# Chunk attention and a phase MLP on one core: one copy for q and k, token weights cast in the load queue, and a new order of steps

## The chip, the core and the metric

The kernel runs on one core of a Trainium2 chip. A core has TensorE (PE; its weight loads are shown as PEld), VectorE (DVE), ScalarE (ACT), GpSimd (POOL) and SyncE (SP), and 16 DMA engines. POOL issues the loads that change the type on their way (the software queue), SP issues stores, plain copies inside SBUF and DMA transposes. The metric is device time in microseconds of one execution; the median over runs of the same program is compared.

## The reference

For batch 8, 8 heads, 576 positions and head size 64, attention is taken inside chunks of 64 positions. Its output x, 576 x 512 for each batch, goes through a layer that mixes tokens by two weight matrices and channels by one:

```python
scores = scale * np.matmul(q_c, k_c.transpose(0, 1, 2, 4, 3))   # chunks of 64
attn = softmax(scores)
x = (attn @ v_c), heads joined                                   # (8, 576, 512)
theta = x @ w_theta
zr, zi = x * np.cos(theta), x * np.sin(theta)
y = einsum('ts,bsd->btd', w_tok_r, zr) + einsum('ts,bsd->btd', w_tok_i, zi)
u = x + y
return u + np.maximum(u @ w_ch, 0.0)
```

All inputs and the output are float32. The token product of a batch needs all 576 positions of zr and zi of that batch.

## The kernel before

**Tiling.** Two batches form a pair p (0 to 3). A pair has 9 tiles of 128 rows, numbered 0 to 8: 0 to 3 belong to the first batch, 5 to 8 to the second, and tile 4, the middle, holds the last 64 rows of each. The attention steps work on groups of tiles: A is tiles 0 and 1, B is 2 and 3, C is 5 and 6, D is 7 and 8, M is the middle. A step named S.1C is the score step of pair 1, group C; Y.15 is the token product of pair 1, tile 5. A last number in a step's name is the PSUM slot, three double ones ("wide") and two single ones ("thin").

**Steps.** For a group: `q`, `k`, `v` load in float16 through POOL (two DMAs each, of 128 KB written, or 64 KB for M); `T` transposes q and k on PE into one PSUM tile, `tq` copies the q part and `tk` the k part to SBUF (tq on DVE; tk on ACT, for M on DVE); `S` is the scores, `e` the exponential on ACT; `V0` and `V1` multiply by v for four heads each, with the row sum in an extra column; `v0` and `v1` normalise on DVE; `X` transposes x on PE and `x` copies it on ACT, or `Xd` does both as one DMA transpose from SP; `H` multiplies by w_theta; `g` is cosine and sine on ACT; `z` makes zr and zi on DVE; `zm` moves the odd halves of the middle tile by DMA. For a tile: `Y` is the token product, nine matmuls of 512 columns (`Ya`, `Yb`, `Yc` are parts of it for pair 0, first batch), `y` adds x on DVE to give u; `U` transposes u on PE and `u` copies it (even tiles on ACT, odd on DVE), or `Ud` does it by a DMA transpose; `W` multiplies by w_ch, `w` takes the relu and adds u on DVE, `st` stores with two DMAs from SP.

**Weights.** `lt` and `lc` load w_theta and w_ch in float16. `lw.00` loads the real token weights as float32 by SP into `wraw` and `wend`, and `cw` casts them on ACT into `wnat`; `lw.01` loads the imaginary ones through POOL, where the DMA casts. `TW` transposes them on PE in three parts of 30 blocks, each copied by DVE (`twd`) and ACT (`twa`).

**Order.** The order of all steps is written out in one list, ORDER, and every engine works through its own instructions in that order; an engine that waits holds everything behind it. SP's list holds stores, middle moves and transposes mixed. `D` is an idle step: two matmuls (in the old code) on a blank tile whose result nobody reads. Around the places that the prediction speaks of, the old order reads

```
... v1.0B x.0M H.0M.2 V0.0B.0 x.0A ... TW.01.2 z.0A Ya.01.1 ...
... Xd.3D W.24.0 w.22 w.24 W.25.1 H.3D.0 ...
... W.33.1 w.33 st.36 st.34 st.33 U.38.0 u.38 W.38.1 w.38 st.38 D.00.0
```

**Lines.** In the profile: L157 idle matmuls, L174 loads of q and k, L182 loads of v, L198 and L199 the casts, L225 TW, L241 and L243 its copies, L259 T, L277 and L279 tq and tk, L290 S, L303 e, L323 V0 and V1, L335 and L336 v0 and v1, L354 X, L366 x, L375 Xd, L388 H, L404 and L408 g, L417 and L418 z, L431 and L432 zm, L457 Y, L465 y, L474 U, L482 Ud, L489 and L491 u, L497 W, L506 w, L521 st.

Of the kernel before, what the change touches and what calls it, by code (L numbers as in the profile page):

```python
# [9 lines left out]
FP32 = mybir.dt.float32  # L10
FP16 = mybir.dt.float16
# [7 lines left out]
ones.00 D.00.0 lw.00 cw.00 D.00.1 init.00 D.00.0 D.00.1 q.0M q.0B q.0A D.00.0 k.0M  # L19
D.00.1 D.00.0 D.00.1 k.0B TW.00.0 twa.00 k.0A D.00.0 T.0M.1 tk.0M D.00.1 D.00.0 tq.0M  # L20
S.0M.2 e.0M lt.00 T.0B.1 T.0A.2 tk.0A tq.0B D.00.1 tq.0A tk.0B S.0A.2 v.0M V1.0M.1 v.0A
e.0A D.00.0 V0.0M.2 twd.00 S.0B.0 new.00 v1.0M V1.0A.1 v0.0M V0.0A.2 v0.0A v.0B q.1M
v1.0A lw.01 X.0M.2 e.0B V1.0B.0 X.0A.1 v1.0B x.0M H.0M.2 V0.0B.0 x.0A v0.0B q.0C k.1M
v.0C H.0A.1 g.0M X.0B.0 z.0M zm.0M x.0B g.0A TW.02.2 H.0B.0 T.1M.1 twa.02 twd.02 TW.01.2
z.0A Ya.01.1 tk.1M tq.1M g.0B Ya.03.0 twd.01 S.1M.1 k.0C q.0D z.0B q.1B twa.01 Yb.01
T.0C.0 e.1M Yb.03 tq.0C Yc.03 tk.0C S.0C.2 Yc.01 v.1M y.03 k.0D Ya.02.0 e.0C lc.00
V1.0C.1 new.10 V0.0C.0 Yb.02 y.01 v0.0C Yc.02 v.0D v1.0C U.01.1 X.0C.2 u.01 T.0D.0
V0.1M.1 Ya.00.1 Yb.00 x.0C tk.0D y.02 U.02.0 tq.0D v0.1M V1.1M.2 k.1B v1.1M S.0D.1
H.0C.0 u.02 W.02.0 w.02 e.0D V1.0D.2 q.1D V0.0D.1 Yc.00 v1.0D v0.0D g.0C U.03.0 T.1B.2
X.0D.1 X.1M.0 u.03 q.1A y.00 z.0C x.0D W.03.0 w.03 tq.1B x.1M U.00.1 k.1D u.00 H.0D.1  # L30
W.01.1 w.01 tk.1B g.0D z.0D H.1M.0 S.1B.2 k.1A g.1M T.1D.1 tk.1D q.1C v.1B tq.1D e.1B
v.1A W.00.0 k.1C w.00 z.1M Y.05.1 st.01 T.1A.0 tk.1A Y.07.0 v.1D y.05 tq.1A q.2D V0.1B.1
S.1A.2 S.1D.0 e.1D y.07 U.05.1 u.05 Y.06.0 U.07.1 v0.1B e.1A V1.1A.0 y.06 V1.1B.1 T.1C.2
u.07 tk.1C st.02 st.00 v1.1A U.06.0 u.06 tq.1C v1.1B st.03 Y.08.1 X.1B.0 v.1C V0.1A.2
x.1B S.1C.1 W.05.0 V0.1D.0 y.08 v0.1A e.1C v0.1D X.1A.2 x.1A w.05 U.08.1 zm.1M H.1B.1
W.07.0 H.1A.0 g.1B V1.1D.2 w.07 v1.1D Y.04.0 X.1D.1 q.2M z.1B k.2D q.2C g.1A V1.1C.2
T.2D.0 y.04 x.1D z.1A W.06.0 w.06 k.2M tk.2D H.1D.1 v1.1C st.05 u.08 Y.13.0 tq.2D S.2D.2
v.2C g.1D T.2M.0 k.2C y.13 V0.1C.1 Y.10.1 v0.1C X.1C.1 tk.2M tq.2M q.2A e.2D S.2M.0
st.06 T.2C.2 v.2D y.10 st.07 e.2M x.1C new.20 Y.11.0 q.2B v.2M z.1D q.3A W.08.1 tk.2C
k.2B tq.2C k.2A y.11 w.08 S.2C.0 V1.2D.1 U.11.0 e.2C v1.2D H.1C.2 u.11 V0.2D.0 v0.2D  # L40
V0.2M.1 q.3C g.1C U.13.1 v0.2M st.08 Y.12.0 u.13 W.11.1 y.12 X.2D.0 x.2D w.11 V1.2M.1
k.3A V1.2C.2 v1.2M W.13.0 v1.2C U.10.1 V0.2C.1 v0.2C u.10 T.2B.0 st.11 T.2A.2 tk.2A
tk.2B X.2M.1 w.13 tq.2A W.10.1 z.1C U.04.0 u.04 st.13 w.10 H.2D.2 x.2M k.3C tq.2B W.04.0
w.04 H.2M.1 g.2M Y.17.1 v.3C q.3M T.3A.0 X.2C.1 y.17 g.2D v.2B Y.14.0 st.10 z.2M S.2B.2
x.2C tk.3A tq.3A S.2A.1 S.3A.0 y.14 Ud.17 U.12.1 u.12 Y.18.0 y.18 e.2A Y.16.1 k.3M y.16
e.2B W.17.0 v.2A H.2C.1 e.3A w.17 V1.2A.2 v1.2A V0.2A.0 W.12.1 st.04 zm.2M Y.15.0 v0.2A
Ud.14 v.3D w.12 y.15 g.2C V1.2B.2 v1.2B V0.2B.0 v0.2B q.3B X.2A.1 W.14.1 x.2A Ud.18 w.14
st.17 U.16.0 u.16 T.3C.2 X.2B.1 W.16.0 w.16 tk.3C U.15.1 x.2B H.2A.0 u.15 q.3D k.3B
W.15.0 W.18.1 st.12 T.3M.1 k.3D tq.3C z.2C S.3C.2 w.15 w.18 z.2D tq.3M g.2A e.3C st.14
v.3A H.2B.0 Y.27.0 st.16 new.30 v.3M Y.28.1 z.2A tk.3M g.2B y.28 S.3M.2 y.27 z.2B  # L50
V0.3A.1 T.3B.0 Y.26.1 Y.20.0 tq.3B st.18 v0.3A tk.3B Ud.28 V1.3A.0 y.26 e.3M y.20 v1.3A
V1.3M.2 V1.3C.1 v1.3M v1.3C Y.24.1 V0.3C.0 T.3D.2 st.15 Ud.27 S.3B.1 y.24 tq.3D v0.3C
Ud.26 W.26.0 w.26 e.3B W.27.1 v.3B w.27 tk.3D V1.3B.1 V0.3B.0 v0.3B v1.3B S.3D.2 Ud.20
st.27 W.28.0 w.28 Y.21.1 y.21 Xd.3A Ud.21 Y.25.0 V0.3M.0 st.28 v0.3M y.25 e.3D V1.3D.2
V0.3D.1 st.26 Xd.3M Y.22.1 H.3A.0 Ud.24 v0.3D y.22 v1.3D W.21.0 w.21 W.20.1 H.3M.1 g.3A
Y.23.0 Ud.22 w.20 y.23 W.22.1 g.3M Xd.3B st.21 z.3M st.20 H.3B.2 Ud.25 g.3B Xd.3D W.24.0
w.22 w.24 W.25.1 H.3D.0 w.25 Xd.3C z.3B H.3C.1 z.3A g.3C Ud.23 W.23.0 st.22 w.23 z.3C
g.3D zm.3M Y.32.1 y.32 Y.31.0 z.3D Y.30.1 y.31 Y.37.0 st.24 st.25 y.30 st.23 Ud.30 y.37
Y.35.1 W.30.0 y.35 Ud.31 W.31.1 w.30 Ud.32 Ud.35 Ud.37 w.31 st.30 st.31 Y.36.0 W.35.1
y.36 w.35 W.32.0 w.32 st.35 Ud.36 Y.34.1 y.34 Y.33.0 W.37.1 y.33 W.36.0 w.37 Y.38.1  # L60
st.32 Ud.34 w.36 Ud.33 y.38 st.37 W.34.0 w.34 W.33.1 w.33 st.36 st.34 st.33 U.38.0 u.38
W.38.1 w.38 st.38 D.00.0
# [4 lines left out]
def kernel(  # L67
# [47 lines left out]
    nat = ctx.enter_context(tc.tile_pool(name="nat", bufs=7))  # L115
# [18 lines left out]
    wraw = pairp.tile([P, KT, S], FP32, name="wraw")  # L134
    wend = glob.tile([CH, S], FP32, name="wend")
# [18 lines left out]
    def idle(p, i, slot):  # L154
        ps = psum1("ps_idle", slot)
        for r in range(2):
            nc.tensor.matmul(ps, blank[:, 0:P], blank, start=True, stop=True)  # L157
# [29 lines left out]
    def load_tok(ri):  # L187
        ap = (moe_w_tok_r, moe_w_tok_i)[ri]
        aps = ap[0 : KT * P, :].rearrange("(a p) s -> p a s", p=P), ap[KT * P : S, :]
        if ri == 0:  # L190
            nc.sync.dma_start(wraw, aps[0])
            nc.sync.dma_start(wend, aps[1])
        else:
            nc.gpsimd.dma_start(wnat[:, 0:KT, 1], aps[0])
            nc.gpsimd.dma_start(wnat[0:CH, KT, 1], aps[1])

    def cast_tok():
        nc.scalar.copy(out=wnat[:, 0:KT, 0], in_=wraw)  # L198
        nc.scalar.copy(out=wnat[0:CH, KT, 0], in_=wend)  # L199
# [6 lines left out]
    def tok_w(k3, slot):  # L206
        ps = psum2("ps_wT", slot, FP16)
        for k in range(3):
            kt = 3 * k3 + k
            for tb in range(KT + 1):  # L210
                rows = slice(0, P if tb < KT else CH)
                if tb < KT:
                    at = k * KT * P + (tb // 2) * GT + (tb % 2) * CH
                    to = ps[:, at : at + GT].rearrange("p (c r x) -> p c r x", c=2, r=2)
                    to = to[:, :, 0]
                else:
                    at = 3 * KT * P + k * CH
                    to = ps[:, at : at + CH]
                for h in range(2):
                    if kt < 2 * KT:  # L220
                        ri, jl = kt // KT, kt % KT
                        s0 = (jl // 2) * GT + (jl % 2) * CH + h * P
                    else:
                        ri, s0 = h, KT * P
                    nc.tensor.transpose(  # L225
                        to[half[h]],
                        wnat[rows, tb, ri, s0 : s0 + CH],
                        id16[rows, rows],
                    )
        st["wT", k3] = ps  # L230

    def tok_w_copy(k3, r):
        ps = st["wT", k3]
        ks = slice(3 * k3, 3 * k3 + 3)
        most = ps[:, 0 : 3 * KT * P].rearrange("p (k x) -> p k x", k=3)
        if r == 0:
            c = slice(0, GT)
        else:
            c = slice(GT, KT * P)
        eng = nc.scalar.copy if r else nc.vector.tensor_copy  # L240
        eng(out=wT[:, ks, c], in_=most[:, :, c])  # L241
        if r == 0:
            eng(  # L243
                out=wT[:, ks, KT * P : S],
                in_=ps[:, 3 * KT * P : 3 * S].rearrange("p (k c) -> p k c", k=3),
            )
# [21 lines left out]
    def qk_copy(p, g, which):  # L268
        n = 1 if g == "M" else 2
        ps = st[p]["ps_qkT", g][:, :, which]  # L270
        name = "qk"[which] + "T"
        t = tmp.tile([P, 2, NE, n, CH], FP16, name=name, tag=f"{name}{n}", bufs=n + 1)
        st[p][name, g] = t
        copy = nc.scalar.copy if which and n == 2 else nc.vector.tensor_copy
        if n == 2:
            flat = "p r e j c -> p r (e j c)"
            copy(out=t.rearrange(flat), in_=ps.rearrange(flat))  # L277
        else:
            copy(out=t[:, :, :, 0], in_=ps[:, :, :, 0])  # L279

    def scores(p, g, slot):
        n = 1 if g == "M" else 2
        qT, kT = st[p].pop(("qT", g)), st[p].pop(("kT", g))
        ps = psum2("ps_sT", slot)
        psv = ps.rearrange("p (h j e c) -> p h j e c", h=2, j=2, e=NE)
        for j in range(n):
# [316 lines left out]
```

The softmax here doesn't subtract the row's maximum and nothing guards it: scores larger than these inputs give would overflow.

## Time and profile before

| | |
|---|---|
| median of 8 runs | 212.54 us (211.74 to 213.28) |
| profiled execution | 211.82 us |
| its span | 209.9 us |
| PE busy | 191.0 us, 91% of the span, 2774 matmuls |
| DVE busy | 123.6 us, 59% |
| ACT busy | 111.3 us, 53% |
| POOL busy | 104.3 us, 50%, all of it issuing loads up to 117.5 us |
| first y matmul, end of the last w matmul | 35.83 us, 205.06 us |

The profile is one execution. Its span runs from the first to the last instruction; the execution's own time is 1.92 us longer. A group's row in the page gives line, engine and operation, what it writes and reads, its shape and count, then its busy time and the mean duration of one in ns, then the idle time of the engine just ahead of it with what ended most of that. A matmul's record is longer than its turn: nine y matmuls in a row, of about 380 ns each by their records, take 1.94 us together. So durations on PE are read from the chain of waits, where pieces follow on each other.

### The profile page before, as it was taken

The page shows a single profiled execution, that of the slowest core. Times are in us where ns is not written, and L with a number is a line of the kernel's source. Part 1 is how long each engine was busy: PE and PEld are TensorE (multiplying, and loading weights), DVE is VectorE, ACT ScalarE, POOL GpSimd, SP SyncE. Part 2 cuts the span into 40 slices and gives each one's busy share as a digit, 9 for nine tenths or more (in the row PEclk, how much of TensorE's full clock was granted, in tenths as well). Part 3 has the DMA queues.
Part 4 walks back from the last instruction along what each step waited for, and adds up shares of the span by engine and source line. Part 5 has one row for each costly group of instructions (what it writes and reads, how often), then busy time and mean ns, then how long its engine had stood idle before and what let it go on. Part 6 is the DMA issues. An engine that isn't in the chain of part 4 may idle for free.

```text
span 209.9 us, 6370 instructions
## 1 busy us (share of the span) xinstructions
PE 191.0 (91%) x2774; PEld 96.6 (46%) x2774; DVE 123.6 (59%) x240; ACT 111.3 (53%) x119; POOL 104.3 (50%) x130
## 2 busy tenths in 40 slices
PE   7787698897989999999999999999899979999981
PEld 2335444453545554455555545544544424444430
DVE  0014645564948766676885357949886365846351
ACT  2516487835796678777558668784260631500010
POOL 8997879978999679898899300000000000000000
PEclk9958589999999999999999999999999999999998
DMA  5999999999999999999999993424338687636875
GB/s 190 188 148 172 186 155 162 157 155 154 147 159 200 214 144 169 154 189 157 170 184 198 167 171 91 105 50 87 69 67 170 125 172 148 151 63 129 174 155 128
DMA packets 136859, 31.36 MB, mean 149 GB/s; under 512 B 129537, under 2 KB 131649, under 8 KB 136833
## 3 DMA queue, kind: packets, MB, share of 16 engines
q0 software_dynamic: 114176, 15.88, 117.2%
q1 hardware_dynamic: 22656, 15.10, 31.6%
q8 instruction: 21, 0.34, 0.7%
q14 instruction: 6, 0.04, 0.1%
HBM read 33.06 MB, written 9.44 MB: 202 GB/s over the span
## 4 chain that ended last, share of the span: by engine, by line
PE 65%; DVE 9%; ACT 9%; DMA 7%; POOL 6%; issue 1%; SPq 0%; POOLq 0%; ACTq 0%
PE ps_y L457 27%; PE ps_theta L388 13%; PE ps_uw L497 13%; POOL qk L174 5%; DMA v<-in_v_dram 4%; PE ps_x L323 3%; DMA xT<-x 3%; ACT kT L277 3%; PE ps_qkT L259 3%; PE ps_sT L290 2%; DVE qT L277 2%; DVE x L336 2%; PE ps_xT L354 2%; ACT xT L366 1%; PE ps_uT L474 1%
## 5 line engine op out<-in xcount | busy, mean ns | idle before, releaser
L457 PEld LDWEIGHTS <-wT 128*128 128x128 f16 (+1 forms) x360 | 30.7, 100 | 34.5 <-issue 0.8
L457 PE MATMUL ps_y<-zr,wT 128*128 128x512 f16 (+1 forms) x180 | 44.4, 381 | 0.0
L457 PE MATMUL ps_y<-zi,wT 128*128 128x512 f16 (+1 forms) x180 | 42.0, 379 | 0.0
L465 DVE TENSOR_TENSOR u<-ps_y,x 128x512 f16<-128x512 f32 x36 | 24.7, 690 | 27.9 <-PE ps_y L457 26.4
L497 PE MATMUL ps_uw<-wch,uT 128*128 128x512 f16 x144 | 36.3, 380 | 1.2 <-ACT uT L491 0.7
L174 POOL DMA_DIRECT2D qk<-in_q_dram x40 | 34.4, 879 | 5.5 <-issue 1.4
L174 POOL DMA_DIRECT2D qk<-in_k_dram x40 | 34.0, 872 | 6.0 <-DMA qk<-in_k_dram 2.4
L388 PE MATMUL ps_theta<-wtheta,xT 128*128 128x512 f16 x144 | 35.1, 386 | 1.4 <-DMA xT<-x 1.0
L182 POOL DMA_DIRECT2D v<-in_v_dram x40 | 34.2, 887 | 1.1 <-DMA v<-in_v_dram 0.4
L506 DVE SCALAR_TENSOR_TENSOR o<-ps_uw,u 128x512 f32<-128x512 f32 x36 | 24.8, 689 | 15.9 <-PE ps_uw L497 15.3
L404 ACT ACTIVATE cos<-ps_theta,pihalf 128x1024 f16<-128x1024 f32 (+1 forms) x20 | 20.6, 1032 | 21.4 <-PE ps_theta L388 14.9
L303 ACT ACTIVATE eT<-ps_sT 128x1024 f16<-128x1024 f32 (+1 forms) x20 | 18.5, 939 | 16.7 <-PE ps_sT L290 16.6
L336 DVE TENSOR_TENSOR x<-ps_x,recip 128x512 f16<-128x512 f32 (+1 forms) x40 | 25.5, 638 | 1.4
L388 PEld LDWEIGHTS <-xT 128*128 128x128 f16 x144 | 13.4, 98 | 17.3 <-DMA xT<-x 2.1
L497 PEld LDWEIGHTS <-uT 128*128 128x128 f16 x144 | 13.0, 97 | 16.7 <-DMA uT<-u 1.3
L277 ACT COPY kT<-ps_qkT 128x1024 f16<-128x1024 f16 x16 | 16.1, 1018 | 7.9 <-DVE qT L277 4.4
L366 ACT COPY xT<-ps_xT 128x1024 f16<-128x1024 f16 (+1 forms) x15 | 13.9, 931 | 11.1 <-PE ps_xT L354 11.0
L408 ACT ACTIVATE sin<-ps_theta 128x1024 f16<-128x1024 f32 (+1 forms) x20 | 18.7, 937 | 0.0
L491 ACT COPY uT<-ps_uT 128x512 f16<-128x512 f16 x9 | 5.3, 592 | 24.3 <-PE ps_uT L474 24.2
L277 DVE COPY qT<-ps_qkT 128x1024 f16<-128x1024 f16 x16 | 11.0, 688 | 9.3 <-ACT kT L277 6.6
L259 PE MATMUL ps_qkT<-id,qk 64*128 64x64 f16 x576 | 12.9, 197 | 1.4 <-ACT sin L408 0.8
L335 DVE RECIPROCAL recip<-ps_x 128x8 f32<-128x8 f32 (+1 forms) x40 | 7.9, 196 | 10.1 <-PE ps_x L323 9.8
(43 smaller groups left out, 154.1 us busy)
## 6 DMA issues: line engine op xcount, KB each, us to landing
out_dram<-o SPq DMA_DIRECT2D x72, 128.0 KB, 2.5
qk<-in_q_dram POOLq DMA_DIRECT2D x32, 128.0 KB, 6.3
qk<-in_k_dram POOLq DMA_DIRECT2D x32, 128.0 KB, 6.5
v<-in_v_dram POOLq DMA_DIRECT2D x32, 128.0 KB, 6.7
wraw<-in_moe_w_tok_r_dram SPq DMA_DIRECT2D x1, 1152.0 KB, 6.0
wnat<-in_moe_w_tok_i_dram POOLq DMA_DIRECT2D x1, 576.0 KB, 8.1
qk<-in_q_dram POOLq DMA_DIRECT2D x8, 64.0 KB, 6.3
qk<-in_k_dram POOLq DMA_DIRECT2D x8, 64.0 KB, 6.3
```

The source lines that it names most:

```text
L174: nc.gpsimd.dma_start(nats[p, g][rows, which, r], (q, k)[which][b, :, t0 : t0 + n, :].rearrange("h s d -> s h d"),)
L182: nc.gpsimd.dma_start(v16[rows, slot + r, :, 0:D], v[b, :, t0 : t0 + n, :].rearrange("h s d -> s h d"),)
L259: nc.tensor.transpose(psv[:, r, w, e, j, :], t[half[r], w, j, 2 * e : 2 * e + 2, :].rearrange("s h d -> s (h d)"), id16[half[r], half[r]],)
L277: copy(out=t.rearrange(flat), in_=ps.rearrange(flat))
L336: nc.vector.tensor_tensor(out=st[p]["x"][:, j0 : j0 + n, f * NE * D : (f + 1) * NE * D].rearrange("p c (h d) -> p c h d", h=NE), in0=psv[: ...
L388: nc.tensor.matmul(ps[:, j * DM : j * DM + DM], xT[:, j * NDB + db, :], wtheta16[:, db, :], start=(db == 0), stop=(db == NDB - 1),)
L404: nc.scalar.activation(out=cos[:, 0:n].rearrange("p a e -> p (a e)"), in_=pin, func=AF.Sin, bias=pihalf, scale=1.0,)
L408: nc.scalar.activation(out=sin[:, 0:n].rearrange("p a e -> p (a e)"), in_=pin, func=AF.Sin)
L457: nc.tensor.matmul(ps[rows], wT[:, kt, cols], z[:, jz, :], start=(kt == 0), stop=(kt == 2 * KT),)
L465: nc.vector.tensor_tensor(out=u, in0=st[p].pop(("ps_y", j))[:, 0:DM], in1=st[p]["x"][:, j], op=ALU.add)
L497: nc.tensor.matmul(ps, uT[:, db * P : db * P + P], wch16[:, db, :], start=(db == 0), stop=(db == NDB - 1),)
L506: nc.vector.scalar_tensor_tensor(out=o, in0=st[p].pop(("ps_uw", j)), scalar=0.0, in1=u, op0=ALU.max, op1=ALU.add)
```

## The change

It does five things.

- `tq` and `tk` become one instruction that copies q and k together, 2048 columns of PSUM (1024 for M), on DVE (`tq`, ten of the groups) or on ACT (`tqa`, the other ten).
- Both token weights are loaded through POOL, cast by the DMA, each in two parts: rows 0 to 255 and rows 256 to 575. `cw`, `wraw` and `wend` are gone. `TW` goes in four parts by rows and columns (16, 20, 24 and 30 blocks), all copied by DVE.
- Copies of xT and uT name their engine in the order: `x` and `ua` on ACT, `xv` and `uv` on DVE (xT: four and seven; uT: seven and six).
- DMA transposes: Xd for nine groups (2A to 2D and all of pair 3; before: pair 3) and Ud for 23 tiles (before: 20). In the old order the first of them stands among the steps that load pair 3; in the new one the first is Xd.2B.
- The order is new, an idle step is one matmul, and there are 60 of them (before: 14 steps of two). Buffers: 8 instead of 7 for loaded q and k, 7 instead of 6 for u, 5 instead of 4 for uT, and one ring of 4 for the joint copy.

The new order, cut to its start, the steps around the first DMA transpose, and its end:

```
new.10 lw.01 ones.00 D.00.0 q.0A q.0M D.00.1 D.00.0 D.00.1 D.00.0 D.00.1 lw.00 D.00.0
D.00.1 D.00.0 D.00.1 D.00.0 q.0B init.00 k.0A v.0B D.00.1 TW.00.0 TW.01.1 twd.01 D.00.0
D.00.1 k.0M D.00.0 D.00.1 k.0B D.00.0 D.00.1 v.0M T.0A.2 D.00.0 D.00.1 twd.00 D.00.0
T.0M.1 tqa.0A D.00.1 tq.0M S.0M.0 D.00.0 e.0M D.00.1 D.00.0 D.00.1 v.0A lt.00 T.0B.2
...
v1.0A q.0C D.00.0 V1.0B.0 lw.03 H.0M.2 v1.0B D.00.1 X.0A.1 V0.0B.0 k.0D g.0M D.00.0 k.1M
D.00.1 xv.0A v0.0B H.0A.1 D.00.0 X.0B.0 TW.02.2 z.0M k.0C x.0B D.00.1 q.2M H.0B.0 D.00.0
g.0A z.0A D.00.1 TW.03.1 D.00.0 twd.02 v.1M zm.0M v.0D D.00.1 D.00.0 Ya.00.1 v.0C g.0B
...
y.11 v0.2B Xd.2B W.10.0 Xd.2A e.3M W.13.1 Xd.2D V0.2C.1 T.3D.2 tqa.3D v.3C w.10 Ud.14
w.13 v0.2C Ud.11 Y.17.0 g.2M z.2M H.2B.1 y.17 g.2B Xd.2C z.2B st.10 Ud.18 zm.2M q.3A
...
Y.35.1 W.38.0 y.35 st.36 W.34.1 w.38 st.37 U.35.0 uv.35 W.35.0 w.34 D.00.1 st.38 D.00.1
w.35 D.00.0 D.00.1 st.34 D.00.0 st.35 D.00.1 D.00.0 D.00.1
```

The rest of the diff, cut to its core:

```diff
-    nat = ctx.enter_context(tc.tile_pool(name="nat", bufs=7))
+    nat = ctx.enter_context(tc.tile_pool(name="nat", bufs=8))
...
-        for r in range(2):
-            nc.tensor.matmul(ps, blank[:, 0:P], blank, start=True, stop=True)
+        nc.tensor.matmul(ps, blank[:, 0:P], blank, start=True, stop=True)
...
-    def load_tok(ri):
+    def load_tok(i):
+        part, ri = divmod(i, 2)
         ap = (moe_w_tok_r, moe_w_tok_i)[ri]
-        aps = ap[0 : KT * P, :].rearrange("(a p) s -> p a s", p=P), ap[KT * P : S, :]
-        if ri == 0:
-            nc.sync.dma_start(wraw, aps[0])
-            nc.sync.dma_start(wend, aps[1])
-        else:
-            nc.gpsimd.dma_start(wnat[:, 0:KT, 1], aps[0])
-            nc.gpsimd.dma_start(wnat[0:CH, KT, 1], aps[1])
-
-    def cast_tok():
-        nc.scalar.copy(out=wnat[:, 0:KT, 0], in_=wraw)
-        nc.scalar.copy(out=wnat[0:CH, KT, 0], in_=wend)
+        nc.gpsimd.dma_start(
+            wnat[:, 2 * part : 2 * part + 2, ri],
+            ap[part * GT : part * GT + GT, :].rearrange("(a p) s -> p a s", p=P),
+        )
+        if part:
+            nc.gpsimd.dma_start(wnat[0:CH, KT, ri], ap[KT * P : S, :])
...
-    def tok_w_copy(k3, r):
...
+    def tok_w_copy(i):
+        main, middle = st["wT", i]
+        part = i // 2
+        ks = slice(0, KT) if i % 2 == 0 else slice(KT, 2 * KT + 1)
+        nc.vector.tensor_copy(out=wT[:, ks, part * GT : part * GT + GT], in_=main)
+        if part:
+            nc.vector.tensor_copy(out=wT[:, ks, KT * P : S], in_=middle)
...
-    def qk_copy(p, g, which):
+    def qk_copy(p, g, copy):
         n = 1 if g == "M" else 2
-        ps = st[p]["ps_qkT", g][:, :, which]
...
-        copy = nc.scalar.copy if which and n == 2 else nc.vector.tensor_copy
-        if n == 2:
-            flat = "p r e j c -> p r (e j c)"
-            copy(out=t.rearrange(flat), in_=ps.rearrange(flat))
+        ps, t = st[p]["ps_qkT", g], qk_tile(n)
+        tv = t.rearrange("p (r w e j c) -> p r w e j c", r=2, w=2, e=NE, j=n)
+        if n == 1:
+            flat = "p r w e c -> p (r w e) c"
+            copy(out=tv[:, :, :, :, 0].rearrange(flat), in_=ps[:, :, :, :, 0].rearrange(flat))
         else:
-            copy(out=t[:, :, :, 0], in_=ps[:, :, :, 0])
+            copy(out=t, in_=ps.rearrange("p r w e j c -> p (r w e j c)"))
...
-    def x_copy(p, g):
+    def x_copy(p, g, copy):
...
-    def u_copy(p, j):
+    def u_copy(p, j, copy):
...
-        "tq": lambda p, g: qk_copy(p, g, 0),
-        "tk": lambda p, g: qk_copy(p, g, 1),
+        "tq": lambda p, g: qk_copy(p, g, nc.vector.tensor_copy),
+        "tqa": lambda p, g: qk_copy(p, g, nc.scalar.copy),
```

## The prediction

> **What bounds the kernel now.** First the slices of the page, for the stages.
>
> ```profile
> PE   7787698897989999999999999999899979999981
> DVE  0014645564948766676885357949886365846351
> ACT  2516487835796678777558668784260631500010
> PEclk9958589999999999999999999999999999999998
> DMA  5999999999999999999999993424338687636875
> ```
>
> A slice is 5.25 us. Loads keep the DMA engines full (9) until slice 24, about 126 us. PE is full from slice 10 to the end, apart from thin places. Before slice 7 its digits flatter it: they hold idle matmuls and a clock at 5 or 8 tenths. Then the view by stages, cut where PE begins a piece of work (columns: window, length, PE, PEld, DVE, ACT, POOL busy with counts, granted clock, DMA, GB/s).
>
> ```profile
> 22.44:35.83 13.39, 11.45 (x198) 6.43 (x197) 7.40 (x17) 10.18 (x12) 11.98 (x16) 0.81 2.08 170
> 35.83:62.16 26.33, 23.34 (x450) 12.64 (x449) 16.52 (x34) 17.80 (x21) 23.86 (x28) 1.00 2.29 154
> 87.13:125.32 38.19, 37.57 (x663) 19.86 (x661) 24.08 (x49) 26.35 (x29) 28.18 (x34) 1.00 2.08 177
> 161.00:177.15 16.15, 14.51 (x67) 6.05 (x66) 9.63 (x17) 5.23 (x6) 0.00 (x0) 1.00 0.78 159
> 205.06:209.90 4.84, 0.42 (x2) 0.00 (x0) 0.69 (x1) 0.00 (x0) 0.00 (x0) 0.85 0.56 122
> ```
>
> The first y matmul runs at 35.83 and the last w matmul ends at 205.06. PE loses 3.0 us from 35.83 to 62.16, 0.6 from 87 to 125, 1.6 from 161 to 177; the tail is 4.84. So there is a start-up, then a nearly full PE. The chain of waits tells what the start waits for (start, us, what):
>
> ```profile
> 14.54 7.86 DMA v<-in_v_dram
> ...
> 29.92 1.01 ACT xT L366
> 30.93 1.02 ACT cos L404
> 31.95 0.91 ACT sin L408
> 32.86 0.70 ACT wT L241
> ```
>
> The last v load of the first three groups lands at 22.44; from there ACT is in the way, copies and sines in one queue. The groups the change rewrites:
>
> ```profile
> L277 ACT COPY kT<-ps_qkT 128x1024 f16<-128x1024 f16 x16 | 16.1, 1018 | 7.9 <-DVE qT L277 4.4
> L366 ACT COPY xT<-ps_xT 128x1024 f16<-128x1024 f16 (+1 forms) x15 | 13.9, 931 | 11.1 <-PE ps_xT L354 11.0
> L277 DVE COPY qT<-ps_qkT 128x1024 f16<-128x1024 f16 x16 | 11.0, 688 | 9.3 <-ACT kT L277 6.6
> ```
>
> kT and qT wait for each other across two engines. Last, the DMA transposes of u, from 110 to 125 us and then from 125 to 150:
>
> ```profile
> DMA to landing us min/median/max: 6.2/6.9/8.2
> ...
> DMA to landing us min/median/max: 2.4/2.4/3.0
> ```
>
> Three were issued among the loads (113.8 to 120.4); the last landed at 126.6 or later, where the loads end. Afterwards one takes 2.4, a two-tile xT 3.3.
>
> **Prices on PE**, from the chain's rows at full clock: T 0.57 (M group 0.34), S 0.38 (0.25), half a V pair 0.25 (0.13), X 0.34 (0.22), H 1.73 (0.87), Y 1.94, U 0.25, W 0.87. Added along the old order they give 13.9 us ahead of the first y matmul and 158.2 behind it. The span from there to 205.06 is 169.2, so 11.0 are losses: 3.9 up to 62.16, 2.2 from there to 125.3, 4.9 behind it.
>
> **ACT and DVE.** Per 512 more columns a DVE copy from PSUM grows by 0.27 (418 to 688 ns), an ACT copy by 0.43 (592 to 1018), so the joint copy of 2048 costs 1.23 on DVE (at most 2 x 0.69) and 1.87 on ACT (at most 2.04). ACT loses 16.1 (kT), 10.4 (eleven of fifteen xT), 2.4 (wT), 2.8 (the two casts), 1.2 (two uT) and four of its fourteen table loads at 1.28, 5.1; it gains nine joint copies and one of an M group, 17.9. Net -20: 111 to 91. DVE loses 14.4 (q, k of M), gains seven joint copies and three of M, 10.7, seven xT 4.3, wT 1.2, and drops 0.4: 124 to 125. Only what stands in a chain is worth time. PE's waits that ended on ACT after 38 us were 0.84, 1.4, 0.76, 0.94 and 0.68; I take half of them as saved, 1.5 before 126 and 0.8 after. Not all: between the first Y and T.1A the new order holds 19.3 us of DVE work beside 19.5 of PE, so DVE takes ACT's place there. Bounds: none, or all 4.6.
>
> **PE.** Four X of full groups and three U become DMA transposes: 4 x 0.34 + 3 x 0.25 = -2.1. TW transposes stay 90. Idle matmuls go from 28 to 60: 46 before the second token product, where PE waits anyway, 8 at the very end beside the last relu and store (8 x 0.22 = 1.7, under the 4.84 tail), 6 between; these six cost nothing where PE waits and 1.3 where not. I take nothing.
> The granted clock falls to 5 or 8 tenths in slices 2 to 6, where PE is idle between steps. The Trainium skill, "TensorE: Matmul & The Clock Gate" (the two states), says that the clock halves after about 3.4 us without work and comes back after as much sustained work. By that the scattered idle matmuls would give back about 1 us of a 1.82 us theta step; I count none, as the start is bound by landings.
>
> **The start.** POOL issues at 0.88 per load of a group (two each), 0.70 for M, 0.76 per weight part. In the new order the token parts stand between, the identity after the fifth load step; v.0A is issued at 17.6 and w_theta at 18.4 (before: 17.1 and 12.4). The queue's pace: between the landings of token weight i (28.05) and w_ch (44.8) it moved the worth of seven full load steps (an M step is half) and w_ch, so 2.1 us a step with 2.0 for a weight (an estimate). From 2.8 on, two half weights and 7.5 steps at this pace land v.0A at 20.6; issue plus the median of 6.7 says 24.3. I take 22.6, as before: the 1.33 MB that SP used to move beside it is gone, half of it is put in the queue. From there: DVE norms and xT copies to v0.0B 28.1, H.0A to 29.0, X.0B, xT on ACT to 30.6, cos and sin of A to 32.8, then TW.03, whose PSUM slot they held, to 34.4, idle 0.7, first Ya at 35.1. Bounds 33.1 and 36.8. Old: 35.83. The casts (2.8) and twa (0.8) leave ACT here, but the last TW now stands directly ahead of Y.
>
> **Loads against PE.** At 2.1 a step, T.1C has its k at 54.4 with PE there at 55.2 if it lost nothing, T.1B at 66.0 against 65.2, T.2A at 88.0 against 86.9: each just in time, where in the old order no T waited more than 0.4 for a load after 38 us. Cost 0 to 1; I leave it inside the losses.
>
> **The transposes (the step that decides).** Xd.2B is the first. H.2B stands 80.8 us of PE work behind the first Ya. With the old losses of such a stretch, 6.1 less 1.5, PE wants H.2B at 35.1 + 80.8 + 4.6 = 120.5. V0.2B ends 4.5 us ahead of it; norm 0.9, landing 3.3, so unloaded the transpose is just in time. SP is in order: Xd.2A, Xd.2D, Ud.14, Ud.11 are behind it, 1.23 each. When do loads end? 126.0, less 0.7 (POOL starts earlier), 2.3 (4.3 for SP's token load by the queue's pace, 2.0 put back), and 0 to 3 for three transposes and two stores no longer among them: 121.5 (120 to 126). A transpose among loads lands with their end, so H.2B starts at 122.0. Wait 1.5; bounds 0 and 6.
> The Trainium skill, "DMA: Bandwidth & Descriptors" (SWDGE vs HWDGE vs iDMA), says that each DMA engine serves the queues of both kinds in turn. That would let a transpose take about twice its unloaded time, 5 to 7 us, and end before the loads; the row has 6.2 to 8.2. By the rule H.2B would start at 121 to 124. I go by the row.
> The same skill, "VectorE: DVE Perf Modes" (The three transpose paths), gives a 128x128 block 390 ns on TensorE and 1309 ns by DMA, and advises TensorE where PSUM will do; here the trace has 0.25 on PE for four blocks against 2.4 by DMA. By the rule the change is a loss wherever the landing is waited for.
>
> **The rest.** 75.6 us of PE work from H.2B to the last W, losses 4.9 - 0.8 = 4.1, tail 4.84. Sum 122.0 + 75.6 + 4.1 + 4.8 = 206.5, against 209.9. The profiled execution took 211.82, 1.92 beyond its span, and the median of the runs is 0.72 above it: 206.5 + 1.9 + 0.7 = 209.1.
>
> **Rivals.**
> *The load queue falls behind, and the transposes with it (slower).* POOL ended its last issue at 117.5 with 105.6 of issuing: it lagged 5.5 us at 55 and 10 at 75, waiting for DMAs. If the new order lags as much, T.2A's k is issued at 75.9 + 10 and lands 6.5 later, 92.4 against 86.9; the loads end at 126 + 2.7 of added issuing = 128.7. H.2B at 129; 129 + 75.6 + 4.9 + 4.8 = 214.3, median 216.9. It decides once the loads end after 124. For: the old waits. Against: much of the old lag began with SP's weights.
> *SP is full (no change).* From 118 to 203 SP has 32 transposes at 1.23, 26 stored tiles at 1.22 and 2.4 for the middle: 73.5 of 85 us, 86% (before 73%). From 161 to 177 SP was busy without a gap and PE lost 1.6. Twice that on top of the old 4.9: losses 8, 210.4, median 213.0.
> *ACT was the true bound (more gained).* All 4.6 of its waits vanish, the start comes at 33.5, the loads end at 119: H.2B at 119.2, losses 3.3: 202.9, median 205.5.
>
> **How the numbers follow.** Forecast 0.45, queue behind 0.25, SP full 0.12, more gained 0.18. About 0.5%, 1.1 us, is what a measurement here can tell from no change: faster is below 211.5, slower above 213.6. Faster is the third rival and most of the forecast, 0.61; same is the second and the forecast's upper end, 0.13; slower 0.26. The forecast's own range is 207 to 213 (H.2B at 120 to 126). For eight in ten it reaches down to 204.5 and up to 215.5.
>
> **What would show it.** PE's first y matmul near 35; ACT busy near 91, xT transposes on PE down from 216 to 152 and uT from 64 to 52; the DMA digits falling from 9 at 120 to 122 us; H.2B waiting for its xT for 1 to 2 us; PE's lost time between 36 and 62 under 3. The forecast is wrong if the queue's digits stay at 9 beyond 124, if T or V groups wait for loads by more than 2 us, or if PE waits for uT often after 150.

## The result, and the profile after

The new kernel is slower: 214.96 us (median of 21 runs, 213.10 to 218.19) against 212.84 for the kernel before beside it. The ratio is 1.0095, with a 95% interval of 1.0074 to 1.0117. The forecast was 209.1. The ratio leaves out runs more than 1.5% above the fastest of their kernel, the profiled one among them.

The profiled execution took 216.99 us with a span of 215.2, some 2 us above the median; it is used for where time goes, and the ratios for how much. Which part of the hole shown below belongs to these 2 us is not known. First the slices of its page, 5.4 us each and numbered from 0:

```profile
PE   7097898999997999999999909999999799999994
ACT  2003656736675497599211532856332073300000
PEclk9769999999999999999999985999999999999999
DMA  5999999999999999999999999776658767835576
```

From slice 7 on PE is about as full as before or fuller, apart from a 7 in slices 12 and 31 and from one hole: slice 23 reads 0 where before it read 9, and the granted clock there and behind it reads 8 and 5. The DMA engines stay at 9 through slice 24, to about 134 us (before: to 126). The view by stages has the same columns as before.

```profile
35.60:62.00 26.40, 25.11 (x447) 12.96 (x449) 18.46 (x36) 15.92 (x16) 21.36 (x26) 1.00 1.88 134
123.00:137.00 14.00, 7.77 (x27) 3.01 (x26) 3.75 (x7) 6.32 (x8) 0.00 (x0) 0.76 1.40 130
126.00:128.00 2.00, 0.00 (x0) 0.00 (x0) 1.88 (x5) 0.00 (x0) 0.00 (x0) 0.78 3.23 136
130.00:132.00 2.00, 2.00 (x6) 0.63 (x5) 0.00 (x0) 0.00 (x0) 0.00 (x0) 0.50 1.33 190
210.10:215.20 5.10, 2.21 (x9) 0.67 (x7) 0.69 (x1) 0.00 (x0) 0.00 (x0) 1.00 0.69 150
```

The first y matmul runs at 35.60. Up to 62 PE now loses 1.3 us where it lost 3.0. From 123 to 137 it is busy for 7.8 of 14, and what it does there runs at half clock (third column from the right: 0.50 between 130 and 132). The chain of waits (start, us, what) names the hole:

```profile
118.87 0.70 DVE x L345
...
119.71 9.72 DMA xT<-x
129.43 0.05 issue
129.47 7.54 PE ps_theta L397 x24
```

Xd.2B, the first DMA transpose of pair 2, is issued at 119.71, as soon as DVE has normalised the group, and lands 9.72 us later. PE's timeline (start, busy us, what; in brackets the idle time before it and what ended it) has the wait and the 24 theta matmuls behind it:

```profile
129.47 7.54 PE L397 MATMUL ps_theta<-wtheta,xT 128*128 128x512 f16 x24 [6.23 <-DMA xT<-x]
```

PE waited for 6.23 of the 9.72, and the matmuls take 7.54 us. The transposes of x between 110 and 135 us, by the view of tile xT:

```profile
DMA to landing us min/median/max: 3.1/8.7/10.4
```

The 3.1 is the one issued after the loads. The loads beside them were slow too. The last six of v, by the view of tile v:

```profile
DMA to landing us min/median/max: 6.4/6.9/11.0
```

The last two, issued at 119.7 and 120.6, took 10.0 and 11.0, so the loads end at about 131.6. The groups that the change rewrote (busy, mean ns of one, idle before):

```profile
L278 ACT COPY qkT<-ps_qkT 128x2048 f16<-128x2048 f16 x9 | 16.7, 1869 | 23.4 <-PE ps_qkT L253 23.4
L278 DVE COPY qkT<-ps_qkT 128x2048 f16<-128x2048 f16 x7 | 8.5, 1219 | 2.8 <-PE ps_qkT L253 2.8
```

The joint copies wait for PE alone; the two engines no longer wait for each other.

### The profile page after: what moved, and what is told of

The parts are those of the page before. It is cut to its first block, busy times and chain, and to the rows that moved or that the text cites. A ratio compares the mean times of both kernels' runs of the same rounds, so it can differ in the third digit from the quotient of the medians.

```text
span 215.2 us, 6239 instructions
## 1 busy us (share of the span) xinstructions
PE 193.2 (90%) x2730; PEld 95.2 (44%) x2730; DVE 125.1 (58%) x232; ACT 92.3 (43%) x91; POOL 106.8 (50%) x134
## 4 chain that ended last, share of the span: by engine, by line
PE 55%; DMA 23%; POOL 15%; DVE 2%; issue 2%; SPq 0%; POOLq 0%
PE ps_y L466 23%; PE ps_uw L503 13%; PE ps_theta L397 12%; POOL qk L173 9%; DMA xT<-x 6%; POOL v L181 5%; DMA qk<-in_q_dram 4%; DMA qk<-in_k_dram 4%; DMA wtheta<-in_moe_w_theta_dram 4%; DMA v<-in_v_dram 3%; PE ps_qkT L253 2%; PE ps_x L332 2%; DMA uT<-u 2%; PE ps_sT L299 2%; POOL wnat L191 1%
## 5 line engine op out<-in xcount | busy, mean ns | idle before, releaser
L397 PE MATMUL ps_theta<-wtheta,xT 128*128 128x512 f16 x144 | 36.1, 398 | 7.4 <-DMA xT<-x 7.3
L278 ACT COPY qkT<-ps_qkT 128x2048 f16<-128x2048 f16 x9 | 16.7, 1869 | 23.4 <-PE ps_qkT L253 23.4
L397 PEld LDWEIGHTS <-xT 128*128 128x128 f16 x144 | 13.9, 102 | 25.3 <-DMA xT<-x 8.3
L156 PE MATMUL ps_idle<-blank 128*128 128x512 f16 x60 | 19.3, 424 | 1.4 <-DVE pihalf L144 1.2
L426 DVE TENSOR_TENSOR zr<-x,cos 128x1024 f16<-128x1024 f16 x16 | 10.9, 684 | 8.2 <-ACT cos L413 8.2
L253 PE MATMUL ps_qkT<-id,qk 64*128 64x64 f16 x576 | 12.4, 191 | 2.2 <-DMA qk<-in_k_dram 2.2
L253 PEld LDWEIGHTS <-qk 64*128 64x128 f16 x576 | 9.8, 95 | 7.0 <-DMA qk<-in_k_dram 3.3
L332 PE MATMUL ps_x<-v,eT 64*64 64x65 f16 x576 | 11.3, 195 | 1.5 <-DMA v<-in_v_dram 0.7
```

What stands on the lines that cost most here:

```text
L253: nc.tensor.transpose(psv[:, r, w, e, j, :], t[half[r], w, j, 2 * e : 2 * e + 2, :].rearrange("s h d -> s (h d)"), id16[half[r], half[r]],)
L397: nc.tensor.matmul(ps[:, j * DM : j * DM + DM], xT[:, j * NDB + db, :], wtheta16[:, db, :], start=(db == 0), stop=(db == NDB - 1),)
```

## The experiments

All ratios are against the kernel before, run beside it on the same chip.

### The X groups of pair 2 on PE instead of DMA

```
- y.11 v0.2B Xd.2B W.10.0 Xd.2A ... Xd.2D ...
+ y.11 v0.2B W.10.0 ... X.2B.2 x.2B V0.2C.1 X.2A.2 x.2A ... H.2B.1 X.2D.0 xv.2D ...
```

> The new kernel with the four xT of pair 2 (2A to 2D) transposed on PE and copied by ACT (2B, 2A) and DVE (2D, 2C); all else as in the new order. Theory L, the transposes issued among the loads make H.2B wait: the wait of 6.2 us before H.2B goes, the theta matmuls behind it run at full clock again (7.5 to about 5.2 us for 24), and PE gains 4 x 0.34 = 1.4 of transposes: 7 us less than the new kernel, a ratio to the kernel before near 0.977. Theory S, SP's list or the rest of the new order is what costs: PE finds another wait of several us within 10 us of the old place, and the time stays within 2 us of the new kernel, ratio 1.00 to 1.01.

Measured: ratio 1.0039 (1.0009 to 1.0070), span 211.6. The hole is gone, and others came. From PE's timeline:

```profile
122.75 1.90 PE L397 MATMUL ps_theta<-wtheta,xT 128*128 128x512 f16 x8
125.53 1.89 PE L397 MATMUL ps_theta<-wtheta,xT 128*128 128x512 f16 x8 [0.55 <-ACT qkT L278]
128.84 1.89 PE L397 MATMUL ps_theta<-wtheta,xT 128*128 128x512 f16 x8 [1.08 <-DVE xT L375]
158.45 1.04 PE L503 MATMUL ps_uw<-wch,uT 128*128 128x512 f16 x4 [1.77 <-DMA uT<-u]
202.99 1.90 PE L503 MATMUL ps_uw<-wch,uT 128*128 128x512 f16 x8 [1.45 <-DMA uT<-u]
```

H.2B starts at 122.75 at full clock, 6.7 us earlier. But PE now does the four X (1.4 us at the forecast's price), waits 2.5 us for copies (0.91 before X.2A, and the 0.55 and 1.08 shown) and 3.2 for two uT. So the span fell by 3.6 and the measured time by about 0.6%. The ratio lies where theory S put it and far from the 0.977 of theory L: closing the hole in this way gave back far less than its length. Which theory names the cause of the wait is decided by the next experiment.

### Ten v loads of pair 3 left out

```
- ... v.3D ... v.3C ... v.3M ... v.3A ... v.3B
+ (none of them)
```

> The new kernel without the ten loads of v for pair 3 (its attention uses the v of pair 1 that lies in the same buffer). The transposes stay. Theory L: the loads end 4.5 steps x 2.1 = 9.5 us earlier, at about 118.5, so Xd.2B, issued at 119.7, lands in 3.3 us and H.2B waits under 1 us; ratio near 0.975. Theory S (the transposes are slow by their size and their number in SP's list, loads or not): Xd.2B takes more than 7 us again, ratio above 1.00.

Measured: ratio 0.9872 (0.9819 to 0.9925). It leaves out work that the other kernels do. POOL's last issue ends at 110.4 instead of 121.5. From PE's timeline:

```profile
122.82 3.41 PE L397 MATMUL ps_theta<-wtheta,xT 128*128 128x512 f16 x15 [1.49 <-DMA xT<-x]
```

With all DMA transposes kept, the wait falls from 6.23 to 1.49. So most of the landing hangs on the loads, and not on SP's list as it stood in the new kernel. But not all of it: Xd.2B was issued 7.4 us after POOL's last issue had ended, the load queue moved nothing between 116 and 122.77, and the transpose still took 4.98 us. From the chain of waits:

```profile
117.79 4.98 DMA xT<-x
```

The expectation had 3.3 and a wait under 1 us. Three transposes were issued one behind the other here (5.0, 4.6 and 4.0 us); a later one took 3.0. Why the first of a row takes so long is not shown.

### The hole filled with idle matmuls

```
- w.13 v0.2C Ud.11 Y.17.0 g.2M z.2M H.2B.1
+ w.13 v0.2C Ud.11 Y.17.0 (26 x D.00.1) g.2M z.2M H.2B.1
```

> The new kernel with 26 idle matmuls (5.6 us at full clock) ahead of H.2B, where PE stands idle. If the half clock behind the wait comes from the idle PE, the 24 theta matmuls take 5.2 instead of 7.5 us and the kernel gains 1.5 to 2.3 us (ratio near 1.000); H.2B itself starts as late as before, near 129.5. If the clock has another cause, they still take 7.5 us and the ratio stays near 1.010.

Measured: ratio 1.0341 (1.0261 to 1.0422). From PE's timeline:

```profile
121.64 11.17 PE L156 MATMUL ps_idle<-blank 128*128 128x512 f16 x26
132.66 5.34 PE L397 MATMUL ps_theta<-wtheta,xT 128*128 128x512 f16 x24
```

I had sized the fill at half of what it took: written into one PSUM slot, each idle matmul holds PE for 0.43 us. As a remedy it failed. It still prices the clock: with PE kept busy the granted clock stayed at 1.00 and the 24 theta matmuls take 5.34 us, with the hole 7.54. The hole cost 2.2 us more than its length.

### The stores before H.2B left out

```
- st.00 ... st.08, st.16 (each two stores of 128 KB from SP)
+ (left out)
```

> The new kernel without the stores of the ten tiles that come ahead of the first DMA transpose (01 to 08 but for 04's neighbours in pair 0 and 1 and tile 16 as listed in the order): their outputs are not written. My sum assumed that transfers from SP slow the loads. If so, 2.6 MB less beside them end the loads 2 us or more earlier (POOL's last issue at 119 or before, H.2B 2 us earlier). If the loads go at a pace of their own queue, POOL's last issue stays within 1 us of 121.5 and H.2B within 1 us of 129.5.

One execution: 209.74 us, span 208.0. POOL's last issue ends at 116.75, 4.8 us earlier, and H.2B waits 1.50. As far as one execution can tell, what SP moves in the midst of the loads slows them, by 0.2 to 0.5 us for each tile of 256 KB. The lower end compares with the kernel with X on PE (118.84), the upper with the new kernel (121.50).

### The real token weights by SP and ACT again

```
-        nc.gpsimd.dma_start(wnat[:, 2 * part : 2 * part + 2, ri], ...)
+        if ri == 0:
+            if part == 0:
+                nc.sync.dma_start(wraw, ...)
+                nc.sync.dma_start(wend, ...)
+            return
...
+    "cw": cast_tok on ACT, at the start of the order
```

To make room, `new.10` is moved later and eT has four buffers instead of five. All else is the new kernel.

> The new kernel with one part undone: the real token weights come again over SP's queue as float32 and ACT casts them, as in the kernel before; the load queue is spared its weight steps. By the forecast's price (SP's load cost the load queue 4.3 us, the cast load 2.0) the loads must end 2.3 us later than in the new kernel: POOL's last issue at 123.8 instead of 121.5, H.2B at 131.8 instead of 129.5, ratio about 1.02. By the price that the early stores gave (0.2 to 0.5 us for a tile of 256 KB that SP moves beside the loads, so 1.0 to 2.4 us for 1.33 MB, less 2.0) the loads end between 1 us earlier and 0.4 later: POOL's last issue between 120.5 and 121.9, H.2B within 1 us of 129.5, ratio 1.005 to 1.012.

Measured: ratio 0.9956 (0.9922 to 0.9990), span 209.3: faster than the kernel before by 0.4%, and outside what either price had allowed. POOL's last issue ends at 116.79 instead of 121.50. The chain of waits:

```profile
119.66 4.75 DMA xT<-x
124.41 0.05 issue
124.45 5.35 PE ps_theta L408 x24
```

Xd.2B is issued within 0.05 us of the time in the new kernel, and lands in 4.75 instead of 9.72. H.2B starts 5.0 us earlier, after a wait of 1.27, and its 24 matmuls run at full clock. The last two v loads took 5.8 to 5.9 us instead of 10.0 and 11.0. Where the load queue loses its time is seen at the load of w_ch, which stands behind all token weights and behind the same loads of q, k and v in both kernels. POOL's timeline of the new kernel, then of this one:

```profile
45.41 0.83 POOL L199 DMA_DIRECT2D wch<-in_moe_w_ch_dram  x1
```

```profile
41.15 0.81 POOL L210 DMA_DIRECT2D wch<-in_moe_w_ch_dram  x1
```

Over the kernels of this study with the same loads ahead of it, w_ch is issued at 43.7 to 45.7 where the queue casts the real weights (eight kernels, median 44.8) and at 40.8 to 41.4 where SP loads them (four, median 41.2). The two groups don't overlap. Moving this load onto the queue costs the queue 3.6 us net; the forecast had it gaining 2.3.

### SP's load taken away from the kernel before

```
-            nc.sync.dma_start(wraw, aps[0])
-            nc.sync.dma_start(wend, aps[1])
+            nc.vector.memset(wraw, 0.0)
+            nc.vector.memset(wend, 0.0)
```

> The kernel before, with SP's load of the real token weights left out (1.33 MB; DVE fills its buffer with zeros instead, so the real part of the token product is left out; the casts on ACT and all else stay). It prices the disputed term by itself. By the forecast's price that load costs the load queue 4.3 us: POOL's last issue comes at about 113.2 instead of 117.5. By the reading of the kernel with the token load put back (the load had landed 6 us after its issue, before the queue was full) it costs nothing: POOL's last issue stays within 1 us of 117.5, and only the first weight transposes, which waited for it, come earlier; ratio 0.985 to 1.0.

Measured: ratio 1.0015 (0.9986 to 1.0045). The same row of POOL's timeline, of the kernel before and then of this one:

```profile
36.44 0.83 POOL L202 DMA_DIRECT2D wch<-in_moe_w_ch_dram  x1
```

```profile
36.45 0.76 POOL L202 DMA_DIRECT2D wch<-in_moe_w_ch_dram  x1
```

At w_ch, long after SP's load has landed, the queue stands where it stood. So by this row SP's load cost it 0, with an uncertainty of about 2 us (the spread of this row among like kernels), and not 4.3. POOL's last issue does end 2.9 us earlier, at 114.57, between what the two readings expected. Kernels with the same loads as the new one differ in that row by as much (118.8 to 121.7), so it is not evidence for SP's load, but it doesn't rule out a cost of up to 2.9 either. The time did not move, so in the kernel before little can have hung on when the loads ended.

### The joint copy undone

```
-            copy(out=t, in_=ps.rearrange("p r w e j c -> p (r w e j c)"))
+            for which, eng in ((0, nc.vector.tensor_copy), (1, nc.scalar.copy)):
+                eng(out=tv[:, :, which]..., in_=ps[:, :, which]...)
```

On top of the kernel with X of pair 2 on PE.

> The kernel with the X groups of pair 2 on PE, and the joint copy of q and k undone: for the eight-row groups DVE copies q and ACT copies k, as before. If ACT is no bound (the forecast's chain of PE), ACT's busy time rises by 4 to 8 us, DVE's falls, and the time moves by less than 0.5%: ratio 1.000 to 1.009. If ACT was the true bound (third rival), PE waits on ACT again between 36 and 62, and the ratio is 1.015 or more; a ratio below 0.999 would mean that DVE's one long copy costs more than it spares.

Measured: ratio 1.0370 (1.0312 to 1.0429), against 1.0039 with the joint copies. That is the side on which ACT binds, though not by its total: its busy time hardly moved, 94.2 to 93.4 us, where I had expected 4 to 8 more. What counts is that one step needs two engines again. From PE's timeline and the view by stages:

```profile
46.23 0.45 PE L334 MATMUL ps_x<-v,eT 64*64 64x65 f16 x32 [1.70 <-ACT eT L314]
71.43 0.32 PE L301 MATMUL ps_sT<-qkT 64*64 64x64 f16 x16 [1.85 <-ACT qkT L276]
72.36 0.43 PE L334 MATMUL ps_x<-v,eT 64*64 64x65 f16 x16 [0.61 <-ACT eT L314]
```

```profile
62.00:72.00 10.00, 7.86 (x158) 3.99 (x157) 4.46 (x9) 6.33 (x7) 9.90 (x12) 1.00 2.18 183
72.00:80.00 8.00, 7.59 (x150) 3.92 (x149) 2.56 (x5) 2.30 (x4) 6.92 (x9) 0.58 2.46 155
```

Between 36 and 62 PE loses 1.9 us, where it lost 0.03 with the joint copies. It loses 2.1 us between 62 and 72, and the clock is then down to 0.58 for 8 us, which costs about 7.59 x 0.42 = 3.2 more (an estimate). The waits ahead of that, 1.85 and 0.61 us, are far shorter than the 6.23 of the new kernel. This order was found for joint copies, so the 3% are the copy's worth in this order, not by itself.

### The middle idle matmuls, the late waits, and the single gains together

Three attempts at a version that beats both. The first drops six idle matmuls from the kernel with X on PE; in the new kernel's profile they lie between 41 and 84 us, not 37 and 62 as the expectation says.

```
- T.0C.0 tq.0C D.00.0 Yb.00 ... k.1B w.01 tqa.1A Y.07.1 tq.1C D.00.0 S.1C.2 ...
+ T.0C.0 tq.0C Yb.00 ... k.1B w.01 tqa.1A Y.07.1 tq.1C S.1C.2 ...
```

> The kernel with the X groups of pair 2 on PE, less the six idle matmuls that the new order has in the middle (between 37 and 62). If PE no longer waits there, each costs what it lasts, 0.35 to 0.43 us: 2.1 to 2.6 us in all, of which 1 to 2.2 reach the end: ratio 0.994 to 0.999. If they lay in waits, or kept the clock up, the ratio stays at 1.004 or rises and the clock of that window falls.

Measured: ratio 1.0005 (0.9974 to 1.0036), against 1.0039 with them. The difference, 0.3% or 0.7 us, is at the edge of what can be told. H.2B starts at 122.77, where it started with them (122.75).

The second also transposes U.26 and U.38 on PE and moves X.2A, T.3D and H.2C apart from the copies that they wait for.

```
- ... Ud.26 v1.3D ... V1.3B.1 ... Ud.38 ...
+ ... v1.3D ... U.26.1 ua.26 V1.3B.1 ... U.38.0 uv.38 ...
```

> The same without the six idle matmuls, and with the last waits on SP's list met: U.26 and U.38 transposed on PE instead of by DMA, and X.2A, T.3D, H.2C and H.2D moved apart from the copies that they wait for. The waits that the kernel with X on PE still shows sum to 5.8 us (0.91, 0.55, 1.08, 1.77, 1.45); two U groups on PE cost about 0.8 us each. If PE's chain sets the end, 3 to 6 us go: ratio 0.975 to 0.99. If DVE or ACT becomes the bound, the waits return elsewhere: ratio 0.995 to 1.005.

Measured: ratio 0.9991 (0.9959 to 1.0023): nothing further. The waits for uT by DMA were gone from its profile; PE waited for loads of k (2.4 us in all), for a sine on ACT (1.8) and for DVE near the end (0.46 and 1.11) instead.

The third takes the first and puts the real token weights back on SP.

```
- new.10 lw.01 ones.00 ... lw.00 D.00.0
+ lw.00 cw.00 lw.01 ones.00 ... D.00.0
```

> The new kernel with three parts undone together: token weights by SP and ACT as before, the X groups of pair 2 on PE, the six idle matmuls in the middle dropped. If the load queue's two weight steps and the transposes among the loads are what made the new kernel slower, the single gains should add up in part: H.2B without a DMA wait near 123.5, POOL's last issue near 116.8, ratio 0.985 to 0.995. If DVE and ACT copies of the four X groups now bound PE, it stays at the 0.996 of the kernel with the token load alone.

Measured: ratio 0.9968 (0.9941 to 0.9994). The gains do not add: 0.9956 with SP's load alone. PE's timeline of this kernel shows what stands in the place of the transposes:

```profile
125.75 1.89 PE L408 MATMUL ps_theta<-wtheta,xT 128*128 128x512 f16 x8 [0.55 <-ACT qkT L289]
129.06 1.89 PE L408 MATMUL ps_theta<-wtheta,xT 128*128 128x512 f16 x8 [1.08 <-DVE xT L386]
158.10 1.04 PE L514 MATMUL ps_uw<-wch,uT 128*128 128x512 f16 x4 [1.20 <-DMA uT<-u]
```

The transpose's wait was down to 1.27 us; the copies that replace it are waited for longer (0.55 and 1.08), and PE has the four X to do besides.

### Fewer idle matmuls at the start

```
- e.0M D.00.1 D.00.0 D.00.1 v.0A lt.00 T.0B.2 D.00.0 V0.0M.1 ...
+ e.0M v.0A lt.00 T.0B.2 V0.0M.1 ...
```

In the kernel just described, 22 fewer.

> The same, less the 22 idle matmuls between the first S group and the first y matmul (they hold about 8 us of PE's chain there). If they stand on PE's path, the first y matmul comes 1.5 to 4 us earlier (from 36.9) and the loads become the bound: ratio 0.975 to 0.99. If they keep the clock up, as their place suggests, the granted clock between 18 and 36 falls toward half, the theta groups take longer and the first y matmul comes no earlier or up to 1 us later: ratio 0.99 to 1.0.

Measured: ratio 0.9965 (0.9928 to 1.0002). Both expectations came true in part. The first y matmul comes at 35.66 instead of 37.14, although the clock between 18 and 36 us falls (0.89 with, 0.67 without). At the end nothing is left of it: between 62 and 90 PE is busy for 26.12 us instead of 27.24.

The same trim, and no middle idle matmuls, with the DMA transposes kept and the real token weights on SP: the forecast's case without its failed term.

```
+ lw.00 cw.00 lw.01 ones.00 ...
- e.0M D.00.1 D.00.0 D.00.1 v.0A ... T.0C.0 tq.0C D.00.0 Yb.00 ...
+ e.0M v.0A ... T.0C.0 tq.0C Yb.00 ...
```

> The new kernel with the real token weights by SP and ACT again, the X groups of pair 2 left to DMA transposes, and no idle matmul from the first S group to the end of the pass (29 fewer; those at the very start and the very end stay). This is the forecast's own case without its failed term: the loads end early enough for the transposes. If idle matmuls stand on PE's path and the loads allow it, the first y matmul comes at about 35.7, H.2B waits 1 to 2 us for its transpose and starts at 123 to 124, ratio 0.985 to 0.995. If the end is held by the loads and by SP's list instead, whatever PE gains at the start is spent in longer waits for xT and uT: ratio 0.994 to 0.999, as without this edit.

Measured: ratio 0.9978 (0.9949 to 1.0008). Row of the view by stages, of the kernel with SP's load alone and then of this one:

```profile
62.00:90.00 28.00, 27.68 (x592) 14.68 (x591) 17.33 (x34) 19.88 (x21) 26.16 (x32) 1.00 2.18 187
```

```profile
62.00:90.00 28.00, 24.63 (x504) 13.02 (x504) 15.87 (x31) 16.98 (x19) 25.37 (x32) 1.00 2.15 181
```

PE starts on y at 36.35 instead of 36.94 and has no fill in the middle; in this stretch it is then idle for 3.4 us instead of 0.3, 1.33 of these behind a load of q. H.2B starts at 124.02, against 124.45. The ratio is the one of the second expectation: what PE gains at the start is spent in later waits. In this stretch the one named is for a load of q, and not for xT or uT as expected; for the longest, 1.54 us ahead of 73.47, the profile names no cause.

## Why the prediction was wrong

**Right in the main: the mechanism.** "A transpose among loads lands with their end" is close to what happened: Xd.2B landed at 129.43, the last loads at 129.7 and 131.6. In three experiments the loads end earlier, by fewer loads (wait 1.49), fewer stores beside the loads (1.50) and the weight load off the queue (1.27), each against 6.23. Two things were missing. The forecast took 3.3 us for a transpose without loads beside it; the first of the row took 4.75 to 5.03 in these three kernels, though their loads had landed 2.6 us or more before it did. So the 1.49 is the forecast's 1.5 by luck: there it stood for loads ending at 121.5. And the loads were held up as well: the last two took 10.0 and 11.0 us beside the transposes, and 5.8 to 5.9 in the kernel with the weight load on SP. Of the forecast's own signs of failure, the digits of the DMA engines beyond 124 us came. The waits of T and V groups for loads passed 2 us only added up (2.3); none was above 1.

**The step that failed: when the loads end.** The forecast had 126.0 - 0.7 - 2.3 and 1.5 more, the middle of its "0 to 3", which makes 121.5. The last load is issued at 120.6 and lands at about 131.6, 10 us later than that. Two terms behind the 2.3 had the wrong size. SP's token load was priced at 4.3 us of queue time, a residual left when other loads had been subtracted from a stretch; taking it away moved w_ch by 0 and POOL's last issue by 2.9. "2.0 put back" for the cast load was too little: the move costs 3.6 net. So "2.3 earlier" should have been about 3.6 later, an error of 5.9. Moving this one load back brought H.2B from 129.47 to 124.45, 5.0 of the 7.5 us by which it came late (forecast 122.0). How the 3.6 divide between the two loads is known only to about 2 us. Nor did the 1.5 for transposes no longer among the loads come: three of the new ones stood beside the last loads. A better sign was at hand: the weight part writes 0.66 MB, as much as 2.5 load steps of 256 KB, which at the forecast's own 2.1 us a step makes 5.3, not 2.0 (an estimate from those numbers).

**Not priced: what stands behind the wait.** Behind the wait of 6.2 us the granted clock was 0.50, which cost 2.2 us more.

**Right: the copies and the start.** ACT fell to 92.3 (forecast 91), DVE rose to 125.1 (125), the joint copies took 1.22 and 1.87 (1.23 and 1.87), the first y matmul came at 35.60 (35.1), and PE's loss up to 62 fell by 1.7 (forecast 1.5, up to 126). PE reached H.2B at 123.2 rather than 120.5: 0.5 comes from the start, and waits for k and v came to 2.3, where the forecast left 0 to 1 inside the losses. What the middle idle matmuls add is not shown; dropping them from the kernel with X on PE left H.2B where it was.

**The sum.** 129.47 to H.2B, 80.6 to the last W (forecast 79.7; without the 2.2 of the clock, 78.4), 5.1 of tail: 215.2 against 206.5. Of the 8.7, H.2B has 7.5. This is the profiled execution; the median run lies 5.9 above the forecast.

**The rivals.** The slower one, "the load queue falls behind, and the transposes with it", gave loads ending at 128.7, H.2B at 129 and a span of 214.3: H.2B and the span came true almost to the number in the profiled execution, while its median of 216.9 was 1.9 too high. That is in part luck, for its cause was not the one it named. Waits on the way, T.2A 5.5 us late, did not come; the queue fell behind with the cast weights at the start. "SP is full" fell with the experiment that left the loads out and SP's list in. "ACT was the true bound" did not come true (first y matmul 35.60 against its 33.5, loads ending at 131.6 against 119). Still, ACT's copies stand in PE's way: undoing the joint copy in the new order costs 3%, more than the 2.3 us that the forecast gave ACT's waits, and a good part of it is the clock.

**Without the failed term.** With the load back on SP the change is worth 0.4% of the time instead of 1.6%. Its H.2B is at 124.45 against 122.0, and of these 2.45 us the first y matmul (36.94 against 35.1) has 1.8. The casts stand in ACT's queue again, and PE runs at a clock of 0.66 between 12 and 24 us (0.90 in the new kernel). That the rest of the expected gain is held by the pace of the loads is what the two kernels with fewer idle matmuls suggest; no run sped up the whole queue.

**The rules cited.** By the Trainium skill, "DMA: Bandwidth & Descriptors" (SWDGE vs HWDGE vs iDMA), queues are served in turn, which I had read as 5 to 7 us for a transpose; among the loads it took 9.72, so the row, with its 6.2 to 8.2, was the better guide. The same page (Issuing engines are not separate DMA queues) says that the issuing engine saves only issue time, usually small. Here POOL's issue grew by 1.9 us (104.9 to 106.8), but the queue fell 3.6 behind; the measurement decides. "VectorE: DVE Perf Modes" (Rules for kernel authors) advises TensorE where a result in PSUM will do: this case agreed where the landing was waited for 6.2 us (1.0095 to 1.0039), and not where it was 1.3 (0.9956 to 0.9968, no gain).

## What to carry to other kernels

When a transfer moves from one queue to another, price it by where a later load in the same queue is issued, before and after, not by a residual of a stretch with several unknowns. Here a load that ran before the busy queue had filled cost it nothing that w_ch shows, the same weights inside the queue put everything behind them 3.6 us back, and DMA transposes beside that queue landed about when it ended. A wait of PE is to be priced with the half-clock stretch that can follow it (2.2 us here), and closing it gives back only what the next wait leaves.

## What was not expected of the hardware

- DMA transposes of x from SP took 8.7 us (median) among the cast loads, 4.0 to 5.0 three in a row with no load beside them, and 3.0 to 3.1 later. The loads beside them took 10.0 and 11.0 instead of 5.8 to 5.9. Two stores of 128 KB each beside the loads held these up by 0.2 to 0.5 us, by one execution.
- With PE idle from 123.2 the granted clock fell at about 127 (0.78 between 126 and 128) and was back at full by 134 (0.52 between 132 and 134), 4.5 us after PE had begun again. The Trainium skill, "TensorE: Matmul & The Clock Gate" (the two states), has about 3.4 us for either step; here it was 3.9 and 4.5. The clock also fell behind waits of no more than 1.85 and 0.61 us (0.58 between 72 and 80 us, with the joint copy undone). At the start, dropping 22 idle matmuls lowered the clock from 0.89 to 0.67, yet the first y matmul came 1.5 us earlier.
- Idle matmuls that all write one PSUM slot took 0.43 us each at a granted clock of 1.00. The same matmuls in alternating slots take half of that, as three of them ahead of the first y matmul at 35.60 show:

```profile
34.94 0.82 PE L156 MATMUL ps_idle<-blank 128*128 128x512 f16 x3
```
